# A decode block on one core: the first loads of `wq` and `x` are put in another order and cut differently

## Chip, cores and metric

The kernel runs on 1 core of one Trainium2 chip. The metric is the device time of one execution in microseconds (us), lower is better. The time before is the median of 3 runs.

## The reference, cut to what matters

One decode step for 4 sequences: attention over a cache of 8192 positions with 32 heads, beside a SwiGLU feed-forward block, both on the same normalised row, summed with the input. All inputs are bf16.

```python
B, Sq, D = 4, 1, 512;  H, Sk, Dh = 32, 8192, 128;  F = 1792
xn = layernorm(x)                                   # x: (4, 1, 512)
q  = (xn @ wq).reshape(B, Sq, H, Dh)                # wq: (512, 4096)
p  = softmax(einsum("bhqd,bhkd->bhqk", q, k_cache) * Dh**-0.5)
o  = einsum("bhqk,bhkd->bhqd", p, v_cache)          # caches: (4, 32, 8192, 128) each
out = x + o.reshape(B, Sq, H*Dh) @ wo + (silu(xn @ w_gate) * (xn @ w_up)) @ w_down
```

The two caches hold 537 MB of the 551 MB that the profile counts as read; `wq` and `wo` are 4.19 MB each, the three feed-forward weights 1.84 MB each, and `x` 4 KB.

## The kernel before

The work is cut into 32 tiles of 4 heads (`NT`). Each tile has one K block and one V block of 8.39 MB, laid out as 128 partitions with 64 KB each. Three buffers of that size, `slot[0]` to `slot[2]`, hold them in turn. Every transfer is issued by SyncE (SP) on one queue, in the order of the program; a transfer into a slot waits, on SP, for what still reads the slot, and everything behind it on SP waits too.

For a tile, VectorE transposes the K block in place in groups (`turn_k`, L263), TensorE makes the scores in `sps` (`score`, by way of `mm`, L73), the softmax runs on VectorE and ScalarE (`max_1`, `max_2`, `pt_turn`), and TensorE multiplies the probabilities of the tile before with its V block (`pv`, into `oacc`). The loop goes over three tiles at a time and the schedule is written out by hand (`manual_schedule`). After the loop, `wo` is loaded in eleven pieces (`load_wo`, L383, and `load_wo_heads`, L387), multiplied piece by piece, and 4 KB are written out (L453).

The change is in the prologue. Before the first K block is worked on, this happens:

- `wq` is loaded into the front of `slot[2]`, 32 KB in each of 128 partitions (L102 and L103, in a loop over two ranges of partitions, 0 to 15 and 16 to 127). Row group p of `wq` goes to partition p.
- `x` is loaded behind the columns of `wq` in the same slot: its first three rows by L104, its fourth row, as two halves, by L105. `x_sb` is this view.
- the first K block goes to `slot[0]` (`load_k(0, 0)`, L95).
- VectorE converts `x_sb` (L158, which waits for both transfers of `x`), takes mean and variance (L160 to L174), TensorE transposes the result (L179), and 32 matmuls against `wq` make the queries (L73, tile `xps`, from `xnt_w`). VectorE turns them (L195) into `qtn`.
- `load_ffn` (L221 to L223) puts the feed-forward weights where `wq` was, so its first transfer waits for the matmuls of the queries; behind it on SP stand the second K block (L95, into `slot[1]`) and the first V block (L98, into `slot[0]`, after the first K block's scores).
- GpSimd clears the rest of `slot[2]` (L375) once `qtn` is made, and VectorE builds the first `zq` (L257) from `qtn`.

Of the kernel before, what the change touches and what calls it, by code (L numbers as in the profile page):

```python
# [15 lines left out]
def kernel(  # L16
# [13 lines left out]
    nc = tc.nc  # L30
    P = nc.NUM_PARTITIONS

    B, Sq, D = A_x.shape
    _, H, Sk, Dh = A_k_cache.shape
# [3 lines left out]
    EC = D // P  # L38
# [43 lines left out]
    wq_t = slot[2]  # L82
    free = [EC * H * Dh]

    def beside_wq(parts, w, dtype=dt.bfloat16):

        n = w * (2 if dtype == dt.float32 else 1)
        c0 = free[0]
        free[0] += n
        assert free[0] <= SLOT  # L90
        ap = wq_t[0:parts, c0:c0 + n]
        return ap.bitcast(dt.float32) if dtype == dt.float32 else ap
# [5 lines left out]
        nc.sync.dma_start(out=slot[s][:], in_=v_all[bass.ds(n, 1), :, :].rearrange("o p f -> (o p) f"))  # L98

    x_sb = beside_wq(B, D)  # L100
    wq_src = A_wq.rearrange("(p c) n -> p (c n)", c=EC)
    for p0, p1 in ((0, 16), (16, P)):  # L102
        nc.sync.dma_start(out=wq_t[p0:p1, 0:EC * H * Dh], in_=wq_src[p0:p1, :])  # L103
    nc.sync.dma_start(out=x_sb[0:B - 1, :], in_=x_flat[0:B - 1, :])  # L104
    nc.sync.dma_start(out=x_sb[B - 1:B, :].rearrange("b (k e) -> b k e", k=2),  # L105
                      in_=x_flat[B - 1:B, :].rearrange("b (k e) -> b k e", k=2))
    load_k(0, 0)
# [85 lines left out]
    for half in range(NH):  # L193
        for r in range(2):
            nc.vector.transpose(out=qt[:, half, :, r, :],  # L195
                                in_=q_ps[half][:].rearrange("p (x i r) -> p x i r", x=8, r=2)[:, :, :, r])
# [285 lines left out]
```

## Time and profile before

| What | Value |
|---|---|
| time, median of 3 runs (lowest to highest) | 1288.41 us (1288.31 to 1288.48) |
| time of the profiled execution | 1288.41 us |
| its span in the profile | 1286.6 us |
| read from memory, mean rate over the span | 550.77 MB, 428 GB/s |
| share of 16 DMA engines on SP's queue | 99.6% |
| busy: TensorE, its weight loads, VectorE | 54%, 24%, 61% of the span |
| busy: ScalarE, GpSimd | 2%, 1% |
| mean granted TensorE clock | 0.779 of full speed |

The span runs from the first to the last instruction on the core; the 1.8 us that the execution's time has beside it lie around the program. The share of the DMA engines is the time that the packets took against 16 engines over the span; it says that the engines had packets, not that these moved at the best rate. The rates put a packet's bytes where the packet starts, so rates of stretches of a few packets are coarse.

### The profile page before, as it was taken

The page shows a single profiled execution, that of the slowest core. Times are in us where ns is not written, and L with a number is a line of the kernel's source. Part 1 is how long each engine was busy: PE and PEld are TensorE (multiplying, and loading weights), DVE is VectorE, ACT ScalarE, POOL GpSimd, SP SyncE. Part 2 cuts the span into 40 slices and gives each one's busy share as a digit, 9 for nine tenths or more (in the row PEclk, how much of TensorE's full clock was granted, in tenths as well). Part 3 has the DMA queues.
Part 4 walks back from the last instruction along what each step waited for, and adds up shares of the span by engine and source line. Part 5 has one row for each costly group of instructions (what it writes and reads, how often), then busy time and mean ns, then how long its engine had stood idle before and what let it go on. Part 6 is the DMA issues. An engine that isn't in the chain of part 4 may idle for free.

```text
span 1286.6 us, 11915 instructions
## 1 busy us (share of the span) xinstructions
PE 695.2 (54%) x4507; PEld 307.2 (24%) x4507; DVE 789.0 (61%) x743; ACT 28.9 (2%) x70; POOL 13.1 (1%) x12
## 2 busy tenths in 40 slices
PE   1565456654456654456654456654456654456656
PEld 0232122222222221222222122222222221222223
DVE  2976556666556666556666556666557666557662
ACT  0000000000000000000000000000000000000000
POOL 1200000000000000000000000000000000000000
PEclk9987688777778776788777788867788776788867
DMA  9999999999999999999999999999999999999998
GB/s 294 432 427 445 425 435 438 428 438 438 428 436 440 428 436 438 430 436 438 430 434 436 434 432 434 436 432 434 438 426 438 438 428 438 438 428 436 438 422 349
DMA packets 11705, 550.90 MB, mean 428 GB/s; under 512 B 1320, under 2 KB 1840, under 8 KB 2736
## 3 DMA queue, kind: packets, MB, share of 16 engines
q1 hardware_dynamic: 11696, 550.78, 99.6%
q8 instruction: 6, 0.10, 0.0%
q14 instruction: 3, 0.02, 0.0%
HBM read 550.77 MB, written 0.00 MB: 428 GB/s over the span
## 4 chain that ended last, share of the span: by engine, by line
PE 48%; DVE 22%; another core or an unknown queue 14%; DMA 9%; issue 5%; DVEq 0%; PEld 0%; SPq 0%; ACT 0%; PEldq 0%
PE sps L73 36%; DVE slot L263 12%; PE oacc L73 9%; DMA slot<-in_A_k_cache_dram 7%; DVE ptz L293 4%; DVE zq L257 2%; PE xps L73 2%; DVE oacc L325 2%; DMA slot<-in_A_x_dram 2%; DVE o L326 2%; PE mps L73 1%; PE mps L279 1%; DMA slot<-in_A_wo_dram 0%; DVE rcp L302 0%
## 5 line engine op out<-in xcount | busy, mean ns | idle before, releaser
L73 PE MATMUL sps<-slot,zq 128*128 128x512 bf16 x2048 | 516.5, 416 | 394.2 <-DVE slot L263 394.2
L263 DVE STREAM_TRANSPOSE slot<-slot 128x2048 uint32<-128x2048 uint32 (+1 forms) x194 | 561.5, 2958 | 209.2 <-DMA slot<-in_A_k_cache_dram 209.2
L73 PEld LDWEIGHTS <-zq 128*128 128x128 bf16 x2048 | 211.1, 103 | 687.5 <-issue 348.6
L293 DVE STREAM_TRANSPOSE ptz<-p__118 32x512 bf16<-32x512 bf16 x128 | 89.9, 703 | 87.0 <-PE mps L73 84.0
L73 PE MATMUL oacc<-slot,ptz 128*16 128x512 bf16 x2112 | 131.4, 392 | 6.3 <-issue 4.1
L73 PE MATMUL xps<-rowy,o 128*128 128x4 f32 x66 | 18.4, 350 | 157.7 <-DVE o L326 157.7
L274 DVE TENSOR_REDUCE mx<-sps 128x1 f32<-128x512 f32 x32 | 22.1, 692 | 99.5 <-PE L73 62.2
L73 PEld LDWEIGHTS <-ptz 128*16 128x16 bf16 x2112 | 59.0, 112 | 64.7 <-issue 24.8
L73 PEld LDWEIGHTS xps<-rowy,o 128*128 128x128 f32 x66 | 16.2, 304 | 160.3 <-issue 110.8
L287 ACT ACTIVATE p__118<-sps,nb 128x512 bf16<-128x512 f32 x32 | 22.0, 687 | 1169.5 <-PE oacc L73 768.4
L257 DVE COPY zq<-qtn 32x4 bf16 (+1 forms) x128 | 29.9, 234 | 3.5
L325 DVE TENSOR_TENSOR oacc<-oacc,rowu 128x512 f32<-128x512 f32 x33 | 23.1, 700 | 8.1 <-PE L73 7.1
L326 DVE TENSOR_REDUCE o<-oacc 128x128 f32<-128x512 f32 x33 | 22.8, 692 | 1.1
L282 DVE TENSOR_REDUCE nm<-mps 128x4 f32<-128x64 f32 x32 | 7.2, 225 | 22.6 <-PE L73 22.6
L321 DVE TENSOR_TENSOR otn_nat<-xps,rcp 128x4 f32 (+1 forms) x33 | 5.4, 163 | 24.1 <-PE xps L73 22.0
L73 PEld LDWEIGHTS mps<-rowb,rs 128*128 128x128 f32 x64 | 9.5, 186 | 13.2 <-issue 13.2
L73 PE MATMUL mps<-rowb,rs 128*128 128x4 f32 x64 | 12.3, 263 | 0.0
L73 PE MATMUL yo_ps<-slot,ident 4*4 4x256 bf16 x2 | 0.4, 368 | 22.0 <-DMA slot<-in_A_x_dram 22.0
L158 DVE CAST slot<-slot 4x512 f32<-4x512 bf16 x1 | 0.4, 416 | 18.9 <-DMA slot<-in_A_x_dram 18.9
L279 PE MATMUL mps<-ident_f,mx 128*128 128x128 f32 x32 | 10.3, 323 | 0.0
L375 POOL MEMSET slot<- 128x11264 bf16 x1 | 9.5, 9486 | 27.6 <-DVE qtn L202 27.6
L279 PEld LDWEIGHTS mps<-ident_f,mx 128*128 128x128 f32 x32 | 4.3, 133 | 13.2 <-DVE mx L274 12.4
(60 smaller groups left out, 68.7 us busy)
## 6 DMA issues: line engine op xcount, KB each, us to landing
slot<-in_A_v_cache_dram SPq DMA_DIRECT2D x1, 4096.0 KB, 44.9
slot<-in_A_v_cache_dram SPq DMA_DIRECT2D x2, 2048.0 KB, 51.0
slot<-in_A_wq_dram SPq DMA_DIRECT2D x1, 3584.0 KB, 21.2
slot<-in_A_wo_dram SPq DMA_DIRECT2D x7, 512.0 KB, 18.6
slot<-in_B_w_gate_dram SPq DMA_DIRECT2D x1, 1792.0 KB, 17.1
slot<-in_B_w_up_dram SPq DMA_DIRECT2D x1, 1792.0 KB, 20.0
slot<-in_B_w_down_dram SPq DMA_DIRECT2D x1, 1792.0 KB, 22.9
slot<-in_A_wq_dram SPq DMA_DIRECT2D x1, 512.0 KB, 7.0
```

Source lines behind the costliest of these rows:

```text
L73: nc.tensor.matmul(out_ap, lhsT=lhsT, rhs=rhs, start=start, stop=True, skip_group_check=True, **kw)
L257: nc.vector.tensor_copy(out=zq[q0:q1, :, XO + a * QB], in_=qtn[q0:q1, bass.ds(n * 4, 4)])
L263: nc.vector.transpose(out=ap, in_=ap)
L274: nc.vector.reduce_max(out=mx[:], in_=sps[:], axis=AX.X)
L279: nc.tensor.matmul(mps[:, 0:P], lhsT=mx[:, 0:1].to_broadcast([P, P]), rhs=ident_f[:, :], is_transpose=True, start=True, stop=True, skip_gr ...
L282: nc.vector.tensor_reduce(out=nm[:], in_=by_row(mps[:, 0:P]), axis=AX.X, op=ALU.max, negate=True)
L287: nc.scalar.activation(out=p_[:], in_=sps[:], func=ACT.Exp, bias=nb[:, 0:1], scale=qscale, accum_out=rs[:])
L293: nc.vector.transpose(out=ptz[y * QB:(y + 1) * QB, :, y, :, :].rearrange("p s u x -> p s (u x)"), in_=p_[y * QB:(y + 1) * QB, :].rearrange ...
L321: nc.vector.tensor_tensor(out=otn_nat[:, bass.ds((n + 1) * HT, HT)], in0=xps[:], in1=rcp[c % NSLOT][:], op=ALU.mult)
L325: nc.vector.tensor_tensor(out=o_, in0=o_, in1=rowu[:].unsqueeze(2).to_broadcast([P, NV, Dh]), op=ALU.mult)
L326: nc.vector.reduce_sum(out=o1[:], in_=o_.rearrange("p u d -> p d u"), axis=AX.X)
L375: nc.gpsimd.memset(slot[2][:, w3:SLOT], 0.0)
```

## The change

The first three rows of `x` are issued ahead of `wq` instead of behind it. `wq` is loaded by one transfer over all 128 partitions instead of one over 16 and one over 112. The fourth row of `x` and the first K block stay behind `wq`. One transfer fewer is issued; nothing else in the order of any engine's instructions differs, apart from which semaphore each transfer uses.

```diff
     x_sb = beside_wq(B, D)
-    wq_src = A_wq.rearrange("(p c) n -> p (c n)", c=EC)
-    for p0, p1 in ((0, 16), (16, P)):
-        nc.sync.dma_start(out=wq_t[p0:p1, 0:EC * H * Dh], in_=wq_src[p0:p1, :])
     nc.sync.dma_start(out=x_sb[0:B - 1, :], in_=x_flat[0:B - 1, :])
+    nc.sync.dma_start(out=wq_t[:, 0:EC * H * Dh], in_=A_wq.rearrange("(p c) n -> p (c n)", c=EC))
     nc.sync.dma_start(out=x_sb[B - 1:B, :].rearrange("b (k e) -> b k e", k=2),
                       in_=x_flat[B - 1:B, :].rearrange("b (k e) -> b k e", k=2))
     load_k(0, 0)
```

## Prediction

> **What bounds the kernel now.** I began with the chain of waits, which gives PE 48% of the span and suggests a TensorE kernel. The next parts of the page say otherwise:
>
> ```profile
> DMA  9999999999999999999999999999999999999998
> GB/s 294 432 427 445 425 435 438 428 438 438 428 436 440 428 436 438 430 436 438 430 434 436 434 432 434 436 432 434 438 426 438 438 428 438 438 428 436 438 422 349
> ...
> q1 hardware_dynamic: 11696, 550.78, 99.6%
> ```
>
> The DMA engines hold packets in every slice from the first to the last, and from the second slice on they move 422 to 445 GB/s. The bytes are fixed, so the kernel ends when 550.8 MB have gone through. Only two slices lag: the last, which is the tail, and the first with 294 GB/s. A slice is 32.2 us, so against 434 GB/s the first is short of 140 x 32.2 = 4.5 MB, which is 10.4 us of transfer. The change works in that slice.
>
> Next I asked for busy time by stretches (columns: stretch, length, busy time of PE, PEld, DVE, ACT and POOL, then clock, DMA share, GB/s).
>
> ```profile
> 8.00:20.00 12.00, 0.00 (x0) 0.00 (x0) 0.00 (x0) 0.00 (x0) 0.00 (x0) 1.00 1.01 262
> 20.00:22.00 2.00, 0.03 (x2) 0.06 (x2) 0.06 (x1) 0.00 (x0) 0.00 (x0) 1.00 1.52 526
> 22.00:40.00 18.00, 4.25 (x38) 1.38 (x38) 13.50 (x20) 2.05 (x3) 8.06 (x1) 1.00 0.94 408
> 60.00:1270.00 1210.00, 666.34 (x4324) 294.98 (x4323) 752.23 (x701) 25.17 (x65) 0.00 (x0) 0.77 1.00 434
> ```
>
> From 8 to 20 us no engine computes and the DMA engines are fully occupied, yet they move 262 GB/s; later, equally occupied, they move 434. So packets take too long while `wq` is loaded. How long, the DMA view of single stretches tells (packets, MB, share of 16 engines); in order, 0 to 5, 5 to 8, 8 to 20, 22 to 40 and 1252.9 to 1260 us:
>
> ```profile
> q1 hardware_dynamic: 16, 0.52, 73.2%
> ...
> q1 hardware_dynamic: 32, 0.52, 94.6%
> ...
> q1 hardware_dynamic: 96, 3.15, 101.1%
> ...
> q1 hardware_dynamic: 112, 7.34, 94.1%
> ...
> q1 hardware_dynamic: 96, 3.11, 101.4%
> ```
>
> Share x 16 engines x length / packets is the time of one packet. First stretch: 16 packets of 32 KB, the 16-partition transfer, one per engine, 0.732 x 80 / 16 = 3.66 us each. Second: 16 such packets (the other 16 are 4-byte completions), 0.946 x 48 / 16 = 2.84 us. Third: 96 packets, 1.011 x 192 / 96 = 2.02 us. The 112 packets of the second and third are the 112-partition transfer, seven per engine. Fourth, the first K block in 64 KB packets over 128 partitions: 0.941 x 288 / 112 = 2.42 us. Fifth, the last V pieces, again 32 KB packets but over 128 partitions: 1.014 x 113.6 / 95 = 1.21 us (95 of the 96 are data). The same packet size thus takes 1.21 us in a 128-partition transfer and 2.02 to 3.66 us in the two transfers of `wq`.
>
> **The split of `wq` goes.** Each engine now works through 3.66 + 2.84 + 6 x 2.02 = 18.6 us of `wq`. As one transfer over 128 partitions it has eight packets of 1.21 us: 9.7 us. The difference is 8.9 us, and it lies on the path: nothing covers it, because the K block stands behind `wq` on the same engines and they never idle afterwards. Saved transfer time at the front therefore moves every later packet.
>
> [...] My sum uses the rows.
>
> **The issue of a second `wq` transfer goes.** 0.41 us of SP, while the first was moving: nothing.
>
> **Three rows of `x` go ahead.** `wq` is issued later by one small issue. SP's timeline:
>
> ```profile
> 0.75 0.86 SPq L103 DMA_DIRECT2D slot<-in_A_wq_dram  x2
> 1.66 0.35 SPq L104 DMA_DIRECT2D slot<-in_A_x_dram  x1
> 2.05 0.23 SPq L105 DMA_DIRECT2D slot<-in_A_x_dram  x1
> 2.32 0.36 SPq L95 DMA_DIRECT2D slot<-in_A_k_cache_dram  x1
> 28.81 0.35 SPq L221 DMA_DIRECT2D slot<-in_B_w_gate_dram  x1
> ```
>
> L104 takes 0.35 us and 0.04 of gap, so 0.4 us of delay at a moment when the DMA engines have nothing else. This is a cost in full. Below it there is no gain, because L158 and the first matmul wait for the fourth row too, which stays behind `wq`. The upper bound is a small transfer that must be complete before its engines go on: the output of 4 KB, issued at 1283.55, ends the span at 1286.6, so 3.05 us. I take 0.4, since 3 KB are one row each and their engines have a queue behind them, which is the L104 row and not the output's.
>
> [...]
>
> **The first K block's first packets.** In the stretch 20 to 22 us the share of 1.52 is 48.6 us of packets, nearly all from sixteen 64 KB packets: 3.0 us each instead of 2.42. The 0.6 us may come from engines that finish `wq` unevenly, and then it goes; or it is a start-up cost, and then it stays. I count half, 0.3 us gained, bounds 0 and 0.6.
>
> **What could use up the gain.** The norm and the queries stay behind `wq`: L158 starts at 21.94 because `x` lands then, and L221 is issued 6.9 us later, at 28.81. The chain has the same instructions after the change, so it starts about 8.5 us earlier, at 13.4, and issues L221 at 20.3. The K block then keeps the engines busy for 8 x 2.42 = 19.3 us from about 12, until 31.5. L221 has 11 us to spare, as now. Later loads have the same kind of cover, from the list of issues (KB, us to landing):
>
> ```profile
> slot<-in_A_k_cache_dram SPq DMA_DIRECT2D x32, 51.3
> ...
> slot<-in_A_v_cache_dram SPq DMA_DIRECT2D x31, 36.9
> ```
>
> A V block moves in 19.3 us and lands 36.9 after its issue, so 17 us of it are spent queued; a K block queues for 32 us. Compute may lag by that much before the engines run dry, and since compute is started by the landings it moves with them. GpSimd's clearing (L375), which holds VectorE's first `zq` copy for 8.4 us, hangs on `qtn` and moves too. The tail runs from the landing of the last `wo` piece; its TensorE work may meet another phase of the granted clock, which is 0.70 of full speed on average over 1270 to 1287 us. Of the last matmuls of `wo`, eight took 0.60 us and the next eight 1.21, so I allow 1 us either way and take nothing.
>
> **The sum**, against the profiled execution's 1288.41 us (span 1286.6 and 1.8 around it; also the median): -8.9 + 0.4 - 0.3 = -8.8, so 1279.6 us. Its ends: no recovery of 0.6 and 1 us in the tail, -7.5, 1280.9; all of it and the tail in favour, -10.1, 1278.3; with the 3.05 us for `x`, no recovery and the tail against, -4.9, 1283.5. A measurement of this kernel can tell about 0.2%, 2.6 us.
>
> **Rivals.**
>
> *Part of the gain (1281.5 to 1285.8).* The first transfer of a program is slow whatever its shape, or `x` holds three engines for the 3 us. For it: 3.66, 2.84 and 2.02 us fall with time. Against it: within the 112-partition transfer the rate does not rise further, 262 GB/s both from 8 to 14 us and from 14 to 20, and then the K block, over 128 partitions, is at full rate after one packet per engine.
>
> *No change (1285.8 to 1291).* The low rate belongs to `wq` in memory and not to the split. For it: no other load reads this tensor. Against it: it too is 32 KB in a row per partition, like the last V pieces in packet size. It would give 1288.4 + 0.4 = 1288.8.
>
> *Slower.* The long phase runs at a packet time of 2.42 us, and that may depend on how far apart the engines start. `wq` leaves them uneven; an even `wq` lets all sixteen start together, and they could then collide as the K block's first packets seem to. Place: every K and V block, 537 MB. The point from which it decides: 8.8 us are 0.7% of the long phase, so a fall from 434 to 431 GB/s. The price at 425, the lowest of the page's slices ahead of the last two: 537 MB x (1/425 - 1/434) = 26 us, so 1306 us. For it: slices do vary by 5%. Against it: the mean over 60 to 1270 us is 434, and the 2.42 us come back right after the uneven start.
>
> **How the numbers follow.** Full gain 0.77; part of it 0.07; no change 0.05; slower 0.11. The likeliest gives 1279.6. The range from 1278.3 takes in the likeliest's ends and most of the partial case, up to 1285.0. Full and partial gains beyond 2.6 us make faster 0.84, no change 0.05, slower 0.11.
>
> **What would show it.** Right: the stretch from 2 to 12 us holds 128 packets of 32 KB at some 1.2 us; L158 starts near 13.4, L221 is issued near 20.3, the first V block (61.67 now) near 53, and the first slice rises from 294 to above 400 GB/s, with the other slices as they are. Wrong: `wq` packets still near 2 us (memory or start-up), a stretch without packets behind 31 us (cover gone), or 64 KB packets longer than 2.42 us in the long phase.

## The result and the profile after

The changed kernel takes 1280.11 us (median of 6 runs, 1279.94 to 1280.23) against 1288.34 us before (6 runs, 1288.13 to 1288.48): 8.23 us less, ratio 0.9936 with a 95% interval of 0.9923 to 0.9949. The forecast was 1279.6. The profiled execution took 1280.21 us with a span of 1278.4, 8.2 shorter than before.

The page of the changed kernel, the rates by slice and the share of the queue:

```profile
DMA  9999999999999999999999999999999999999998
GB/s 394 437 448 429 427 436 435 437 427 439 431 443 427 439 429 445 427 433 435 441 431 429 439 435 437 427 439 429 445 427 439 429 445 427 433 435 441 431 424 345
...
q1 hardware_dynamic: 11680, 550.78, 99.6%
```

The first slice rose from 294 to 394 GB/s; the others, the last one aside, lie between 424 and 448, where they lay between 422 and 445. 100 GB/s over 32 us are 3.2 MB, which at 434 GB/s is 7.4 us. That is the gain within the blur of a slice's edge: sixteen 64 KB packets, 1.05 MB or 2.4 us, are counted where they start.

The DMA view of single stretches of the changed kernel, from 2.1 to 3, 3.5 to 11 and 12 to 14 us (packets, MB, share of 16 engines):

```profile
q1 hardware_dynamic: 16, 0.52, 220.1%
...
q1 hardware_dynamic: 96, 3.15, 97.0%
...
q1 hardware_dynamic: 34, 1.05, 121.5%
```

Share x 16 engines x length / packets again. The first 32 KB packet of each engine took 2.201 x 14.4 / 16 = 1.98 us. The next six per engine took 0.970 x 120 / 96 = 1.21 us, where the views of before gave 2.84 and 2.02 us. The first 64 KB packets of the K block (16 of the 34; the rest are small) took 1.215 x 32 / 16 = 2.43 us, where they had been at 3.0.

What moved, in the timelines of SP and VectorE. Two lines of before:

```profile
21.94 0.42 DVE L158 CAST slot<-slot 4x512 f32<-4x512 bf16 x1 [18.95 <-DMA slot<-in_A_x_dram]
...
61.67 0.33 SPq L98 DMA_DIRECT2D slot<-in_A_v_cache_dram  x1
```

The same and the issues around them in the changed kernel:

```profile
0.75 0.37 SPq L101 DMA_DIRECT2D slot<-in_A_x_dram  x1
1.17 0.37 SPq L102 DMA_DIRECT2D slot<-in_A_wq_dram  x1
...
20.18 0.34 SPq L219 DMA_DIRECT2D slot<-in_B_w_gate_dram  x1
...
53.03 0.33 SPq L98 DMA_DIRECT2D slot<-in_A_v_cache_dram  x1
```

```profile
13.30 0.41 DVE L156 CAST slot<-slot 4x512 f32<-4x512 bf16 x1 [8.76 <-DMA slot<-in_A_x_dram]
```

The conversion of `x` starts at 13.30 instead of 21.94, the first feed-forward weight is issued at 20.18 instead of 28.81, the first V block at 53.03 instead of 61.67: 8.6 us each. The long phase keeps its rate (busy time by stretches, changed kernel):

```profile
60.00:1261.00 1201.00, 660.94 (x4231) 291.43 (x4227) 748.84 (x693) 24.90 (x64) 0.00 (x0) 0.77 1.00 434
```

In the DMA records the first packets of the K block start 7.8 us earlier, on average over the engines, and the first feed-forward packets behind it 8.3 us earlier. Of these 8.3 us, 8.2 are still there at the end, 1246 us later.

### The profile page after: what moved, and what is told of

Its sections match the earlier page's. It is cut to its first block, busy times and chain, and to the rows that moved or that the text cites. A ratio compares the mean times of both kernels' runs of the same rounds, so it can differ in the third digit from the quotient of the medians.

```text
span 1278.4 us, 11913 instructions
## 1 busy us (share of the span) xinstructions
PE 697.2 (55%) x4507; PEld 307.3 (24%) x4507; DVE 790.5 (62%) x743; ACT 28.8 (2%) x70; POOL 13.1 (1%) x12
## 4 chain that ended last, share of the span: by engine, by line
PE 49%; DVE 22%; another core or an unknown queue 14%; DMA 9%; issue 5%; DVEq 0%; SPq 0%; ACT 0%; PEld 0%; PEldq 0%
PE sps L73 36%; DVE slot L261 12%; PE oacc L73 9%; DMA slot<-in_A_k_cache_dram 7%; DVE ptz L291 4%; DVE zq L255 2%; PE xps L73 2%; DVE oacc L323 2%; DVE o L324 2%; PE mps L73 1%; DMA slot<-in_A_wo_dram 1%; DMA slot<-in_A_x_dram 1%; PE mps L277 1%; DVE rcp L300 0%
## 5 line engine op out<-in xcount | busy, mean ns | idle before, releaser
L277 PE MATMUL mps<-ident_f,mx 128*128 128x128 f32 x32 | 10.5, 327 | 0.0
L73 PE MATMUL yo_ps<-slot,otn 128*4 128x256 bf16 x56 | 7.1, 407 | 1.0 <-DMA slot<-in_A_wo_dram 0.9
```

The source lines that it names most:

```text
L73: nc.tensor.matmul(out_ap, lhsT=lhsT, rhs=rhs, start=start, stop=True, skip_group_check=True, **kw)
L277: nc.tensor.matmul(mps[:, 0:P], lhsT=mx[:, 0:1].to_broadcast([P, P]), rhs=ident_f[:, :], is_transpose=True, start=True, stop=True, skip_gr ...
```

## Experiments

Two theories were to be told apart. The first is that of the prediction: `wq` was slow because of the partitions into which its two transfers were cut, the place of `x` is a small cost, and the DMA queue's cover (transfers still queued on the engines while compute runs) hides everything else in the prologue. The rivals: the number or the unevenness of the transfers counts, the place of `x` does, or the start of the program is slow whatever is loaded. The time of before on the chips of these runs was 1288.63 us for the first four kernels, 1288.50 for the next four and 1288.61 for the last two, so differences against it say more than the times. The six kernels from the halves to the K block ahead of `wq` ran once each, and so did before beside the last four of them: tenths of a microsecond in these times say nothing, and their DMA records decide. The diffs are shortened: `a <- b` is a transfer on SP's queue, each is against the changed kernel, the first against the kernel before.

**One half of the change: `x` ahead, the cut kept.**

```diff
+    x_sb[0:B-1] <- x_flat[0:B-1]            # ahead
     for p0, p1 in ((0, 16), (16, P)): wq_t[p0:p1] <- wq_src[p0:p1]
-    x_sb[0:B-1] <- x_flat[0:B-1]
```

> The three rows of x ahead, but wq still in transfers of 16 and 112 partitions. If the whole gain is the split's, this takes the time of before plus a later start of wq by one small issue (0.4 us): 1288.7 us, with 32 KB packets of wq between 1.7 and 3.7 us. If the place of x is worth something of its own, or if the packets were slow because wq came first on the queue, 1280 to 1285 us.

Measured: 1288.65 us (1288.09 to 1289.05), ratio to before 0.9999 [0.9990, 1.0009]. Of the gain nothing is left. The stretch from 8 to 20 us is what it was before, in the view of stretches of this kernel:

```profile
8.00:20.00 12.00, 0.00 (x0) 0.00 (x0) 0.00 (x0) 0.00 (x0) 0.00 (x0) 1.00 1.02 262
```

**The other half: one transfer, all of `x` behind it.**

```diff
-    x_sb[0:B-1] <- x_flat[0:B-1]
     wq_t[:] <- wq
+    x_sb[0:B-1] <- x_flat[0:B-1]
```

> wq in one transfer over 128 partitions, and all of x behind it. If the place of x is a pure cost of one issue, this takes 0.3 to 0.4 us less than the changed kernel (1280.11 us): 1279.75 us. If the rows ahead help to start the engines (the first 32 KB packets take 2.0 us in the changed kernel, the later ones 1.21), the first packets are longer here and the time is 1280.1 us or more.

Measured: 1279.67 us (1279.59 to 1279.83), ratio to before 0.9931 [0.9914, 0.9947]. That is 8.96 us under the before of its chip, against 8.23 for the whole change; the two times differ by 0.44 us, the befores of the two sets by 0.29. In the DMA records the first feed-forward packets start at 31.76 us on average over the engines, against 32.19 in the changed kernel: 0.43 us, the place of `x`. The engines' first packets are as slow without the rows ahead (1.94 us), so those start nothing up. All the gain is the cut's, and `x` ahead gives a little of it back.

**What about the cut: halves.**

```diff
-    wq_t[:] <- wq
+    for p0, p1 in ((0, 64), (64, P)): wq_t[p0:p1] <- wq_src[p0:p1]
```

> wq in two transfers of partitions 0 to 63 and 64 to 127, x as in the changed kernel. If a transfer is slow because of which partitions it reaches, halves are slow as well, at least as slow as the 112-partition packets (2.02 us): 16 us or more for wq, 1286.5 us or more in all. If the uneven cut of 16 and 112 is what counts, with 8 packets for every engine at 1.21 us, 1280.1 us. [...]

Measured: 1290.60 us, 2.0 us over the before of its chip. The even cut is worse than the uneven one. From 5 to 20 us, in the DMA view of this kernel:

```profile
q1 hardware_dynamic: 110, 3.08, 99.5%
```

94 of these packets are data, so 0.995 x 240 / 94 = 2.54 us each, twice the 1.21 of the whole transfer.

**The same two transfers of 64, from other partitions.**

```diff
-    wq_t[:] <- wq
+    for p0 in range(2): wq_t[p0:P:2] <- wq_src[p0:P:2]
```

> As the halves, but cut into the even and the odd partitions: again two transfers of 64 partitions with the same packets. If it counts which partitions a transfer reaches, and how they lie, this is as fast as one transfer: packets near 1.21 us, 1280.1 to 1280.6 us. If any transfer of fewer than 128 partitions is slow, it is as slow as the halves: 1286.5 us or more.

Measured: 1280.24 us, 8.4 us under before. From 5 to 11 us, in the DMA view of this kernel:

```profile
q1 hardware_dynamic: 96, 2.62, 101.2%
```

80 are data: 1.012 x 96 / 80 = 1.21 us each. Same number of transfers, same packets, same number of partitions as the halves, and twice the speed. So neither the number of transfers nor their size made `wq` slow; it was which of the 128 rows of `wq`, and with them which partitions, go in one transfer.

In all these kernels row group p goes to partition p, so a half of the partitions is also one stretch of 2.1 MB in memory. That the slowness lies in reading such a stretch, and not in the partitions, is a rival that no run of `wq` separates. Other loads speak against it. In the DMA records of before, a feed-forward weight, 1.84 MB in one stretch but into all 128 partitions, takes 0.535 us per 14 KB packet, 429 GB/s over 16 engines. A piece of `wo`, 0.52 MB in one stretch into all 128, takes 0.159 us per 4 KB packet, 412 GB/s. The packets of the halves move at 206 GB/s by the same count.

Why some cuts are slow was not shown. The runs show that a 32 KB packet's time depends on how the 128 rows are cut: 1.21 us in one transfer and in even and odd partitions, 2.54 in halves, 3.66 in partitions 0 to 15 and 2.02 in 16 to 127 (from 8 to 20 us of before). Which partitions the engines write at one moment is not in the trace.

**The small transfer last.**

```diff
-    wq_t[:] <- wq
+    for p0, p1 in ((0, 112), (112, P)): wq_t[p0:p1] <- wq_src[p0:p1]
```

> wq in transfers of 112 and 16 partitions, the small one last (partitions 112 to 127), x as in the changed kernel. The 16-partition packets took 3.66 us when they came first. If that is the cut, they take about 3.7 us here too, and the time is that of before plus 0.4: about 1288.7 us. If part of it is the start of the program (the changed kernel's first packets take 2.0 us instead of 1.21, so 0.8 us), they take 2.9 us or less here and the first round of the 112-partition packets is longer, with nearly the same sum. The packets decide, not the time.

Measured: 1288.68 us, 0.2 over before. The DMA view of this kernel, from 15.25 to 17.5 us, where the 16-partition packets start, and from 18.5 to 22, where the first packets of the K block do:

```profile
q1 hardware_dynamic: 31, 0.52, 152.6%
...
q1 hardware_dynamic: 34, 1.05, 110.5%
```

16 data packets in the first: 1.526 x 36 / 16 = 3.43 us. One of them is the last of the 112 partitions', and one of the small transfer's starts later; its own sixteen took 3.49 us in the DMA records. They are nearly as slow last as they were first (3.66), so that was the cut and not the start of the program. The second line holds more: the K block's first packets took 1.105 x 56 / 16 = 3.87 us with the small packets beside them, 3.83 in the records, instead of 2.42. In this run the transfer cut badly also slows the first packets behind it, by 1.4 us.

**Two transfers by columns.**

```diff
-    wq_t[:] <- wq
+    for c0 in (0, EC*H*Dh//2): wq_t[:, c0:c0+EC*H*Dh//2] <- wq_src[:, c0:c0+EC*H*Dh//2]
```

> wq in two transfers again, but cut by columns: each over all 128 partitions with 16 KB in each, x as in the changed kernel. If the number of transfers costs nothing and only the cut of the partitions does, 1280.1 us, with wq done in the same 10.6 us. If a second transfer has a cost of its own, up to 0.4 us more (one issue of SP), and a hole between the two.

Measured: 1279.87 us, 8.6 us under before. In the DMA records all 16 KB packets but each engine's first two take 0.61 us. The first transfer's last packets end at 7.88 us on average and the second's first start at 7.89, so 0.01 us lies between the transfers and the second costs nothing that shows. In the changed kernel the K block's first packets start as closely behind the last ones of `wq`, 0.01 us on average.

**The norm taken off the wait: all of `x` first.**

```diff
     x_sb[0:B-1] <- x_flat[0:B-1]
+    x_sb[B-1:B] <- x_flat[B-1:B]
     wq_t[:] <- wq
-    x_sb[B-1:B] <- x_flat[B-1:B]
```

> All four rows of x ahead of wq. The norm then runs under the load of wq and the queries start when wq lands, some 5 us earlier than in the changed kernel. If the queue covers the norm (the first feed-forward weight is issued 11 us before the engines would run dry), this gains nothing and costs one more small issue: 1280.4 us. If the norm is on the path, 1275 us.

Measured: 1280.39 us, 8.1 under before, no better than the change. The prologue did move: in SP's timeline of this kernel the first feed-forward weight is issued 4.5 us earlier than in the changed kernel, and the first V block almost when it was (53.03 there).

```profile
15.65 0.33 SPq L219 DMA_DIRECT2D slot<-in_B_w_gate_dram  x1
...
52.66 0.33 SPq L98 DMA_DIRECT2D slot<-in_A_v_cache_dram  x1
```

Compute that was started earlier gained nothing here while the queue was full; it only waited for the K block.

**The cover taken away: the first K block ahead of `wq`.**

```diff
+    load_k(0, 0)
     x_sb[0:B-1] <- x_flat[0:B-1]
     wq_t[:] <- wq
     x_sb[B-1:B] <- x_flat[B-1:B]
-    load_k(0, 0)
```

> The first K block issued ahead of x and wq. The same bytes in another order: x and wq land some 19 us later, near 33 us, and the feed-forward weights are issued near 39.6 us, while the engines run dry near 31.5. If cover of the queue is what hides the norm and the queries, a hole of about 9 us opens there and 1289 to 1293 us follow (the upper end if the first V block is late as well). If the cover is not needed, 1280 us.

Measured: 1289.91 us, 1.4 over before, where the change is 8.2 under it, with the same bytes at the same rates. Busy time by stretches of this kernel:

```profile
22.00:31.00 9.00, 0.00 (x0) 0.00 (x0) 0.00 (x0) 0.00 (x0) 0.00 (x0) 1.00 1.00 433
31.00:32.00 1.00, 0.00 (x0) 0.00 (x0) 0.00 (x0) 0.00 (x0) 0.00 (x0) 1.00 0.01 1
32.00:40.00 8.00, 3.52 (x34) 1.44 (x38) 3.85 (x9) 0.29 (x1) 0.00 (x0) 1.00 0.00 0
```

`wq` is at full rate (433 GB/s), then the engines stand still for 8.6 us (31.7 to 40.3 in the records, on average) while norm and queries run. That is the price of the 6.9 us chain, with the landing ahead of it and the issue behind it, when no K block is queued behind `wq`. A fast `wq` alone is not the gain; a fast `wq` with a queue that stays full is. This run also has 64 KB packets at the start of the program; they took 3.05 us instead of 2.42.

**Both small savings together.** Columns with all of `x` behind, beside a second run of one transfer with `x` behind on the same chip.

```diff
-    x_sb[0:B-1] <- x_flat[0:B-1]
-    wq_t[:] <- wq
+    for c0 in (0, EC*H*Dh//2): wq_t[:, c0:c0+EC*H*Dh//2] <- wq_src[:, c0:c0+EC*H*Dh//2]
+    x_sb[0:B-1] <- x_flat[0:B-1]
```

> Both small savings together: wq in two transfers by columns over all 128 partitions, and all of x behind it. The place of x saved 0.4 us alone (1279.67 against 1280.11 us), the columns 0.2 us (1279.87). If both are separate terms of the same sum, 1279.5 us, with the first packets of 16 KB near 1.2 us. If the columns' 0.2 us was chance, 1279.7 us.

> The kernel with wq in one transfer and all of x behind it, once more, on the same chip as the combination, for a comparison of tenths of a microsecond: 1279.7 us.

Measured: 1279.51 us (1279.34 to 1279.75) and 1279.50 us (1279.28 to 1279.83). The 0.2 us that the columns seemed to save are not there. One transfer with all of `x` behind it is thus the version that beats both kernels, by 9.0 and 9.1 us against before in its two sets of runs and by 0.4 to 0.6 against the change; every one of its eight runs is under the fastest of the changed kernel's, which was not run again beside it.

## Why the prediction was right, step by step

The forecast was 8.8 us less, made of -8.9 for the packets of `wq`, +0.4 for the issue of `x`, -0.3 for the K block's first packets and nothing for the tail. The sum came out at -8.2. The mechanism held, with one term mis-sized and one guessed. The terms, averaged over the 16 engines from the DMA records:

- *Packets of `wq`: -8.1 instead of -8.9.* This is the one term that was mis-sized. I gave all eight packets 1.21 us, the duration of a row from the end of the kernel. Seven had it; the first of each engine took 1.98. No row showed the start of the program without the bad cut, so it could not be read off; that 16 packets of 3.66 us might hold some of it stood only under a rival. The total is 1.98 + 7 x 1.21 = 10.5 us against 18.6. Of the 8.1 us, 1.7 lie in the first packet of each engine and 6.4 in the seven that were the 112-partition transfer's, the 2.84 us of those right behind the 16-partition packets included.
- *Place of `x`: +0.4, as forecast.* The engines' first `wq` packets start 0.36 us later, and the run without it gained 0.4 us. The upper bound of 3.05 us was far off.
- *K block's first packets: -0.6 instead of -0.3.* They fell from 2.99 to 2.42 us, the upper bound of the prediction, which had counted half for want of a row. That this made good 0.3 of the 0.8 us missed above is luck. The 0.6 us was not a cost of starting up, it went with the cut: 2.99 us behind 16 and 112 partitions, 3.83 behind 112 and 16, 2.42 behind one transfer.
- *To here:* the first feed-forward packets start at 32.19 instead of 40.47 us, -8.3.
- *Tail: +0.2, forecast at 0 with 1 us either way.* The last packets of `wo` end 8.4 us earlier. From the first matmul of its last pieces to the issue of the output there are now 2.38 us (1273.00 to 1275.38), 2.15 before (1281.40 to 1283.55); the granted clock was 0.59 of full speed (from 1261 to 1279 us) and 0.70 before (from 1270 to 1287). Each is one execution, and that the clock made the 0.2 us was not shown.

The lines of the tail, two of before and two of the changed kernel:

```profile
1281.40 0.60 PE L73 MATMUL yo_ps<-slot,otn 128*4 128x256 bf16 x8 [0.25 <-DMA slot<-in_A_wo_dram]
1283.55 0.30 SPq L453 DMA_DIRECT2D out_dram<-res  x1
...
1273.00 1.02 PE L73 MATMUL yo_ps<-slot,otn 128*4 128x256 bf16 x8 [0.23 <-DMA slot<-in_A_wo_dram]
1275.38 0.30 SPq L451 DMA_DIRECT2D out_dram<-res  x1
```

The cover held as said: the first feed-forward weight was issued at 20.18 (forecast 20.3) while the K block kept the engines busy until 32. Of the signs named, one was missed: the first slice reached 394 GB/s and not above 400; the slow first packets cost it some 10 GB/s, an estimate from 0.77 us at 434 GB/s in a slice of 32 us. The rivals are out, but for a part of the first. Part of the gain: start-up costs 0.8 us once per engine (1.98 against 1.21 us), and does not make all of `wq` slow. The 1281.5 us at which this rival's range begins are 1.9 us over the forecast; no run shows a term of that size, and the two transfers by columns were 0.01 us apart. No change: `wq` moves at full rate in one transfer (1.21 us per 32 KB), by columns (0.61 per 16 KB), and in even and odd partitions (1.21 per 32 KB). Slower: all 64 KB packets of the changed kernel average 2.419 us in the DMA records, before 2.420, though the engines now enter the long phase within 0.8 us of each other instead of 1.2.

## What to carry over

Ask of a kernel that is bound by transfers how long one packet takes in each stretch, not how busy the engines are: share x engines x time / packets is in the DMA view, and a share of 101% at 262 GB/s was a fault, not a limit: later 100% moved 434. In this kernel cuts by columns, or into even and odd partitions, were free (1279.87 and 1280.24 us against 1280.11), and cuts into ranges of partitions were not (1288.65 to 1290.60): try the former first. While the queue stayed full, time saved in transfers arrived nearly whole at the end (8.2 of 8.3 us) and time saved in compute not at all (4.5 us, and 1280.39); what a queued block covers shows when it is put elsewhere (8.6 us without packets).

## What the runs showed that was not expected

- The first large packet of each engine was slower by 0.6 to 0.8 us at each of three sizes: 16 KB 1.17 against 0.61 us (columns), 32 KB 1.98 against 1.21 (the changed kernel), 64 KB 3.05 against 2.42 (the K block first).
- The slowness of a badly cut transfer outlasted its own records. Behind the 16-partition transfer, whose packets took 3.49 us, the next packets took 3.83 us instead of 2.42, in one run. Why was not tried.
